# Storing w_in's blocks later, loading the second batch's first groups earlier, and v's first block behind them

## The chip, the cores and the metric

One Trainium2 chip, of which the kernel uses one core. The core has five engines with an instruction stream each (PE multiplies matrices, DVE, ACT and POOL work on vectors, SP issues the transfers) and 16 DMA engines. The metric is device time in microseconds (us), from the start to the end of one execution; lower is better.

## The reference

```python
def _attn_ref(q, k, v, tau):                      # B, N, C = 4, 6080, 256
    qn = q / (norm(q, axis=1) + 1e-06)            # over the N rows, for each channel
    kn = k / (norm(k, axis=1) + 1e-06)
    s = kn.transpose(0, 2, 1) @ qn / tau          # 256 x 256 for each batch
    a = softmax(s)                                # rows of s
    return v @ a

def _moe_ref(x, w_in, w_out):                     # x: the 4 * 6080 rows of v @ a
    h = x @ w_in                                  # d_ff = 2048
    g = h - tanh(h)
    return g @ w_out                              # back to 256 channels
```

## The kernel before

For each batch the kernel computes the 256x256 scores of k against q over all 6080 rows, the softmax, and then folds the result into the weights: (v @ a) @ w_in is computed as v @ (a @ w_in). w_in is cut into 8 blocks (s = 0 to 7) of 256 columns; "fold" multiplies a by one block (tiles `ps_w`), and the folded block `f` is used for all of v. The product v @ f is done by seven half-size products (a Strassen scheme; tiles `x`, `y`, `z` collect them), then tanh and the subtraction follow on ACT and DVE (`t`, `gh`, `gl`), and the product with w_out (`ps_o`). Numbers that need more than one pass are held as a high and a low part (`_hi`, `_lo`, `eh` and `el`, `gh` and `gl`), and products are sums of three.

**The start**, to which all of the change belongs. The first batch's scores are 48 steps of 128 rows over 25 groups (group 0 has one step, the last a half-filled one, all others two). A group is one load of q and k, into whichever tiles are unused that early: `vhl`, `gh`, `gl`, `qh`, `ql`. PE multiplies them (`ps_s`), ACT squares them in place, DVE and POOL add the squares up (`acc`). Then come, one behind the other: the sum of the squares over the rows on PE (`ps_n`, 24 short matmuls), the norms on DVE, their spread (`ps_b`), the scaled scores and their maximum (`s`, `nmx` on DVE), the exponentials on ACT, the transposition on PE (`ps_t`), its high and low part (`eh` on ACT, `el` on DVE), the fold of block 0 (`ps_w`), its scaling and splitting (`fx`, `f`), and then the first seven products with v (`x`). v's first block is one load `vraw_0` of 1 MB; ACT and DVE make the seven pairs `v` (through sums `vt`) out of it.

**What PE does meanwhile.** The second batch's scores are there to fill PE: the first `FILLS` = 48 steps of them ("fills") are put wherever PE would have to wait. In the traces they too are `ps_s`. Their groups are loaded into two tiles `qh` (even groups) and two tiles `ql` (odd groups), so that the load of `qh_4` has to wait until the matmuls on `qh_0` are done.

**The weights.** w_in and w_out come as 64-bit numbers. Each of their blocks (eight and eight) is loaded as `raw` (three tiles in turn) and converted: `L331` on ACT, `L336` to `L346` on DVE (`a_wi`, `m_wi`, `a_wo`, `m_wo`), one addition and one subtraction on POOL or DVE, and a cast on ACT. The converted blocks of w_in are stored to memory for the later batches (`wi_d`, `keep_w_in`, L376); blocks 0 to 2 stay in tiles `wi` until their fold, blocks 3 to 6 are converted in tiles that `f` needs later, and are loaded back.

**What sets the order.** The program is a list of operations. A planner (`Plan.order`) gives each an estimated start from costs and dependences and writes them out in that order; on each engine they run strictly in this order. An operation can have a due time, which only decides which of several ready ones comes first, and `after`, which only delays its estimated start: on the chip there is no wait for either. What an instruction does wait for is data and tiles that come free. All transfers are issued by SP, one after the other, on one queue; an issue that waits for a tile holds up all that stand behind it.

```python
LEAD = 6
KEPT = 50.0
FIRST = 3
...
        if i == len(steps) - LEAD:
            scored.append(plan.last_pe)
...
            size=0.26 * groups[g][1], after=scored if b else (), ...
```

`scored` is the matmul of the first batch's scores behind which the planner lets the second batch's first load start, and until now v's first load too (`plan_moving(0, scored)`). `kept[s]` is the store of block s.

Of the kernel before, what the change touches and what calls it, by code (L numbers as in the profile page):

```python
# [37 lines left out]
EARLY = 6  # L38
FILLS = 48
FILL_EVERY = 0.6  # L40
LEAD = 6
KEPT = 50.0
FIRST = 3
PAD = 208
# [167 lines left out]
def act_cost(n):  # L212
    return 0.14 + n * 0.0009


def dve_cost(n):
    return 0.157 + n * 0.00104
# [11 lines left out]
def attn_moe(ctx: ExitStack, tc: tile.TileContext, qk, v4, qkT, tau, w_in, w_out, outT):  # L229
# [43 lines left out]
    def bank(i, name, shape=(P, 512)):  # L273

        return ps_p.tile(list(shape), F32, tag=f"bank{i}", name=name)
# [6 lines left out]
    def products(out, terms, first, last):  # L282

        seq = []
        for (wh, wl), (xh, xl) in terms:
            seq += [(wh, xh)] if wl is None else [(wh, xl), (wh, xh), (wl, xh)]
        for i, (w, x) in enumerate(seq):
            ins = nc.tensor.matmul(  # L288
                out, w, x,
                start=first and i == 0, stop=last and i == len(seq) - 1,  # L290
                skip_group_check=True,
            )
        return ins
# [63 lines left out]
    wi = {}  # L357
# [6 lines left out]
    def convert_w_in(s, tag):  # L364
        def dst():
            if tag == "f":
                f = sb(f_p, "f", [P, 2, NS, P], F32R, f"w_{s}").rearrange("p a n f -> p (a n f)")
                w = wi[0, s] = f[:, 0:2 * KC * FB].rearrange("p (a k f) -> p a k f", a=2, k=KC)
            else:
                w = w_in_tile(0, s)  # L370
            return w[:, 0].rearrange("p k f -> p (k f)"), w[:, 1].rearrange("p k f -> p (k f)")

        return Convert(f"wi{s}", w_in[s], dst)

    def keep_w_in(s):
        nc.sync.dma_start(wi_d[s], wi[0, s].bitcast(F32))  # L376
# [22 lines left out]
    class Attn:  # L399
# [208 lines left out]


        def fold(self, s, i):  # L610
            w = wi.pop((self.b, s))
            pw = self.pw[s] = bank(i, f"ps_w_{self.b}_{s}", (P, KC, FB))
            for m in range(KC):
                ms = slice(m * P, (m + 1) * P)
                products(
                    pw[:, m, :],
                    [((self.eh[:, kk, ms], self.el[:, kk, ms]), (w[:, 0, kk, :], w[:, 1, kk, :])) for kk in range(KC)],
                    first=m == 0, last=m == KC - 1,
                )
# [79 lines left out]
    plan = Plan()  # L699
# [22 lines left out]
    def plan_convert(conv, dst, after=(), due=None, alone=False):  # L722

        adds = ("DVE", dve_cost(WN), nc.vector) if alone else ("POOL", pool_cost(WN), nc.gpsimd)
        raw, c, t = Buf(ring["raw"]), Buf(ring["nt"]), Buf(ring["ob"])
        plan.add("SP", 0.35, conv.load, writes=[raw, dst], after=after, size=0.52, due=due)
        plan.add("ACT", act_cost(WN), conv.magnitude, reads=[raw], writes=[c])
        plan.add("DVE", 0.84 + 0.69, conv.upper, reads=[raw], writes=[c])
        plan.add("DVE", 0.42 + 0.69, conv.lower, reads=[raw, c], writes=[t])
        plan.add(*adds[:2], lambda: conv.add(adds[2]), reads=[t], writes=[c])  # L730
        plan.add("ACT", act_cost(WN), conv.hi, reads=[c], writes=[dst])
        plan.add(*adds[:2], lambda: conv.lo(adds[2]), reads=[c], writes=[dst])

    kept = {}

    def plan_w_in(s, due=None, tag="wi", after=(), alone=False):
        w = wbuf[0, s] = Buf(ring[tag])
        plan_convert(convert_w_in(s, tag), w, after, due, alone)
        w.writers[-1].due = plan.pe_time - 0.5
        kept[s] = plan.add("SP", 0.35, lambda: keep_w_in(s), reads=[w], size=0.52, due=plan.pe_time + (KEPT if s < FIRST else 0.0))  # L740

    def plan_load_w(b, s):
        w = wbuf[b, s] = Buf(ring["wi"])
# [6 lines left out]
    def plan_moving(i, after=()):  # L750
        v = moving[i] = Moving(i // NP, i % NP)
        n = v.n
        raw, t = Buf(ring["vraw"]), Buf(ring["vt"])
        plan.add("SP", 0.35, v.load, writes=[raw], after=after, size=1.05)
        for j in range(3):
            plan.add("DVE", dve_cost(n if j else 2 * n), lambda j=j: v.sums(j), reads=[raw], writes=[t])
        vbuf[i] = {}
        for j in range(7):
            h = Buf(ring["vhl"])
            l = Buf(f"vl{i}_{j}", h)  # L760
            src = t if v.PLACES[j][0] else raw
            plan.add("ACT", act_cost(n), lambda j=j: v.split_hi(j), reads=[src], writes=[h])
            plan.add("DVE", dve_cost(n), lambda j=j: v.split_lo(j), reads=[src, h], writes=[l])
            vbuf[i][j] = h, l
# [294 lines left out]
    scored = []  # L1059
# [8 lines left out]
    def plain_step(b, i, due=None):  # L1068
        g, jj = steps[i]
        if jj == 0:  # L1070
            plain_load(b, g)

        return plan.add("PE", 2 * KC * 0.215, lambda: ats[b].score(g, jj), reads=held[b, g], writes=[scores[b]], due=due, fill=b == 1)
# [23 lines left out]
    for i, (g, jj) in enumerate(steps):  # L1097
        if jj == 0 and g in early:
            plan_w_in(early[g], due=plan.pe_time, tag="wi" if early[g] < FIRST else "f")
        if i == len(steps) - LEAD:  # L1100
            scored.append(plan.last_pe)
        plain_step(0, i)
        if jj == groups[g][1] - 1:
            plain_square(g)
        if i == 8:
            pt = Buf(1)
            plan.add("PE", 0.1, spread_tau, reads=[tau_b], writes=[pt])
            plan.add("DVE", 0.2, take_tau, reads=[pt], port=False)
    after_scores = plan.pe_time

    fills = [plain_step(1, i, after_scores + FILL_EVERY * i) for i in range(FILLS)]

    sq, pn = [Buf(ring["u"]) for _ in range(2)], Buf(1)
    for x in range(2):
        plan.add("ACT", act_cost(GJ * C), lambda x=x: ats[0].take_squares(x), reads=acc[x:x + 1], writes=sq[x:x + 1])
    plan_moving(0, scored)
    plan.add("PE", 12 * 0.22, lambda: ats[0].sum_squares(1), reads=sq + acc[2:], writes=[pn], late=1.0)
    norms, spread, softmax, transpose = plan_softmax(ats[0], pn, scores[0])
    norms()
# [4 lines left out]
    plan_fold(0, 1, 1)  # L1124
    plan_fold(0, 2, 3)
    plan_w_in(EARLY, due=after_scores, tag="f")
    for s in range(NS2):
        plan_convert(convert_w_out(s), wobuf[s], due=after_scores + 10.0 * s, alone=s > 0)
    for s in range(FIRST, NS2):
        task(max(s - 4, 0), "start", lambda s=s: plan_w_in(s, after=[plan.last_pe], alone=True) if s > EARLY else plan_load_w(0, s))  # L1130
# [90 lines left out]
```

## Time and profile before

| | |
|---|---|
| Median of 3 runs | 2171.91 us (2171.20 to 2172.46) |
| Profiled execution, its own time | 2172.06 us |
| Its span | 2170.3 us |
| PE busy | 2160.4 us |
| DVE busy | 1750.3 us |
| ACT busy | 1529.9 us |
| POOL busy | 33.0 us |
| Mean granted TensorE clock | 0.998 of full speed |

The span is the time between the first and the last instruction in the profiled execution; its own time is 1.76 us longer and can be compared with the runs. A busy PE is not always a PE at its full pace: the granted clock has to be read beside it.

### The profile page before, as it was taken

How to read it: one execution, taken by the hardware profiler on the slowest of the kernel's cores; microseconds unless marked ns; L12 is line 12 of the kernel's file. 1: busy time of each engine (PE TensorE's matmuls, PEld its weight loads, DVE VectorE, ACT ScalarE, POOL GpSimd, SP SyncE). 2: the span in 40 equal slices, each digit the busy share in tenths (PEclk: the TensorE clock that was granted, in tenths of full speed). 3: DMA queues.
4: the chain of work that ended last, by engine and by line, in shares of the span. 5: the costliest groups of instructions: out<-in, count | busy, mean ns of one | idle time of the engine just before them, and what ended most of it. 6: DMA issues, size and time to landing. Idle time of an engine off the chain costs nothing.

```text
span 2170.3 us, 28452 instructions
## 1 busy us (share of the span) xinstructions
PE 2160.4 (100%) x10042; PEld 1818.0 (84%) x10042; DVE 1750.3 (81%) x2844; ACT 1529.9 (70%) x2755; POOL 33.0 (2%) x31
## 2 busy tenths in 40 slices
PE   8999999999999999999999999999999999999999
PEld 7888888888888888888888888888888888888887
DVE  8888877888888777778788877877878878778776
ACT  6566778776777777776677767777667766666665
POOL 5100000000000000000000000000000000000000
PEclk9999999999999999999999999999999999999999
DMA  9844444443454444543345445454333342332331
GB/s 389 330 166 154 164 168 148 162 154 105 151 209 151 172 164 168 182 160 140 126 145 187 170 162 189 143 189 167 128 134 128 122 148 88 129 129 93 125 120 53
DMA packets 82783, 342.23 MB, mean 158 GB/s; under 512 B 9042, under 2 KB 13138, under 8 KB 80082
## 3 DMA queue, kind: packets, MB, share of 16 engines
q1 hardware_dynamic: 82642, 340.43, 43.3%
q8 instruction: 79, 1.29, 0.2%
q14 instruction: 62, 0.51, 0.1%
HBM read 281.94 MB, written 58.46 MB: 157 GB/s over the span
## 4 chain that ended last, share of the span: by engine, by line
PE 98%; DMA 1%; DVE 0%; SPq 0%; issue 0%; ACT 0%
PE ps_o L905 48%; PE x L288 24%; PE y L288 12%; PE ps_s L288 6%; PE z L288 6%; PE ps_w L288 2%; DMA qh<-qk_dram 0%; DMA vhl<-qk_dram 0%; PE ps_n L457 0%; DVE m_wi L346 0%; PE ps_b L564 0%; PE ps_t L599 0%; DVE acc L445 0%; DVE a_wi L339 0%; SPq L323 0%
## 5 line engine op out<-in xcount | busy, mean ns | idle before, releaser
L288 PE MATMUL x<-v,f 128*128 128x512 f32 (+1 forms) x2304 | 614.9, 388 | 0.0
L905 PE MATMUL ps_o<-gh,wo_h 128*128 128x512 f32 (+1 forms) x1536 | 596.8, 389 | 0.0
L905 PE MATMUL ps_o<-gh,wo_l 128*128 128x512 f32 (+1 forms) x1536 | 596.3, 388 | 0.0
L845 DVE TENSOR_TENSOR gl<-t,gh 128x512 fp32r<-128x512 f32 (+1 forms) x768 | 513.1, 681 | 57.3 <-ACT gh L841 55.3
L841 ACT CAST gh<-t 128x512 fp32r<-128x512 f32 (+1 forms) x768 | 463.7, 617 | 68.5 <-DVE t L837 61.2
L288 PEld LDWEIGHTS x<-v,f 128*128 128x128 f32 x2304 | 432.4, 188 | 87.4 <-issue 0.3
L905 PE MATMUL ps_o<-gl,wo_h 128*128 128x512 f32 (+1 forms) x1536 | 472.7, 389 | 0.0
L833 ACT ACTIVATE t<-c 128x512 f32<-128x512 f32 (+1 forms) x576 | 361.3, 628 | 134.0 <-DVE c L821 128.8
L837 DVE TENSOR_TENSOR t<-c,t 128x512 f32<-128x512 f32 (+1 forms) x576 | 392.5, 683 | 76.6 <-ACT t L833 69.0
L805 ACT COPY u<-x 128x512 f32<-128x512 f32 (+1 forms) x384 | 223.9, 583 | 236.7 <-PE x L288 235.7
L905 PEld LDWEIGHTS ps_o<-gh,wo_l 128*128 128x128 f32 x1536 | 288.5, 188 | 56.6 <-ACT gh L841 0.2
L905 PEld LDWEIGHTS ps_o<-gl,wo_h 128*128 128x128 f32 x1536 | 288.6, 188 | 55.3
L905 PEld LDWEIGHTS ps_o<-gh,wo_h 128*128 128x128 f32 x1536 | 288.7, 188 | 53.3
L821 DVE TENSOR_TENSOR c<-u,y 128x512 f32<-128x512 f32 (+1 forms) x384 | 261.0, 680 | 85.1 <-ACT u L805 51.4
L288 PE MATMUL y<-v,f 128*128 128x512 f32 (+1 forms) x1152 | 322.1, 388 | 0.0
L288 PEld LDWEIGHTS y<-v,f 128*128 128x128 f32 x1152 | 216.2, 188 | 43.1
L833 ACT ACTIVATE t<-x 128x512 f32<-128x512 f32 (+1 forms) x192 | 113.9, 593 | 114.7 <-PE x L288 113.5
L837 DVE TENSOR_TENSOR t<-x,t 128x512 f32<-128x512 f32 (+1 forms) x192 | 131.6, 685 | 72.9 <-ACT t L833 71.1
L821 DVE TENSOR_TENSOR c<-p,z 128x512 f32<-128x512 f32 (+1 forms) x192 | 130.9, 682 | 69.9 <-PE z L288 65.8
L288 PE MATMUL z<-v,f 128*128 128x512 f32 (+1 forms) x576 | 161.2, 388 | 0.0
L288 PEld LDWEIGHTS z<-v,f 128*128 128x128 f32 x576 | 108.1, 188 | 21.5
L805 ACT COPY p<-x 128x512 f32<-128x512 f32 (+1 forms) x192 | 112.0, 584 | 11.3 <-PE x L288 8.8
(122 smaller groups left out, 1490.4 us busy)
## 6 DMA issues: line engine op xcount, KB each, us to landing
f<-f_d SPq DMA_DIRECT2D x160, 896.0 KB, 4.6
nt<-qkT_dram SPq DMA_DIRECT2D x96, 380.0 KB, 5.7
f_d<-f SPq DMA_DIRECT2D x32, 896.0 KB, 3.8
raw<-qk_dram SPq DMA_DIRECT2D x46, 512.0 KB, 5.5
vraw<-v_dram SPq DMA_DIRECT2D x20, 1024.0 KB, 7.8
outT_dram<-ob SPq DMA_DIRECT2D x80, 256.0 KB, 3.1
wi<-wi_d SPq DMA_DIRECT2D x28, 512.0 KB, 5.4
vhl<-qk_dram SPq DMA_DIRECT2D x14, 512.0 KB, 8.9
```

Of the source, the lines that this page charges most:

```text
L288: ins = nc.tensor.matmul(out, w, x, start=first and i == 0, stop=last and i == len(seq) - 1, skip_group_check=True,)
L805: nc.scalar.copy(self.tiles[to], self.tiles["X"][:, 0:self.n])
L821: nc.vector.tensor_add(self.tiles[i], self.tiles[u], self.tiles[ps][:, 0:self.n])
L833: nc.scalar.activation(self.tiles["t", i], self.tiles[c][:, 0:n], AF.Tanh)
L837: nc.vector.tensor_sub(x, self.tiles[c][:, 0:n], x)
L841: nc.scalar.copy(self.g[i][0], self.tiles["t", i])
L845: nc.vector.tensor_sub(self.g[i][1], self.tiles["t", i], self.g[i][0].bitcast(F32))
L905: nc.tensor.matmul(outs[key + (m,)][:, 0:n], (wo_l if part else wo_h)[:, f, m * P:(m + 1) * P], quad.g[i][x], start=first and j == 0, stop ...
```

## The change

The converted blocks 3 to 7 of w_in get the same late due time for their store as blocks 0 to 2 had (50 us of planned PE time later). `fold` no longer takes the tile out of the list, since a store may now be written out behind the fold. The second batch's first load may be planned behind the matmul that stands nine steps before the scores' end, not six. v's first load is planned behind the ninth fill (`fills[8:9]`).

```diff
-LEAD = 6
+LEAD = 9
...
         def fold(self, s, i):
-            w = wi.pop((self.b, s))
+            w = wi[self.b, s]
...
-        kept[s] = plan.add("SP", 0.35, lambda: keep_w_in(s), reads=[w], size=0.52, due=plan.pe_time + (KEPT if s < FIRST else 0.0))
+        kept[s] = plan.add("SP", 0.35, lambda: keep_w_in(s), reads=[w], size=0.52, due=plan.pe_time + KEPT)
...
-    plan_moving(0, scored)
+    plan_moving(0, fills[8:9])
```

On SP, around the second batch's first load `qh_0` (names are those of the tiles, the number at the end counts tiles; `raw_wo` and `raw_wi` are loads of blocks to convert). Before:

```order
L323 DMA raw_wo_370<-w_out_dram 128x1024
L376 DMA wi_d_96<-wi_0_111 128x1024
L376 DMA wi_d_97<-wi_1_117 128x1024
L323 DMA raw_wo_395<-w_out_dram 128x1024
L323 DMA raw_wi_403<-w_in_dram 128x1024
L465 DMA qh_0_413<-qk_dram 128x512
L465 DMA ql_1_418<-qk_dram 128x1024
L465 DMA ql_3_428<-qk_dram 128x1024
L376 DMA wi_d_100<-w_241 128x1024
L465 DMA qh_2_445<-qk_dram 128x1024
L376 DMA wi_d_101<-w_291 128x1024
L674 DMA vraw_0_459<-v_dram 128x2048
```

And now:

```order
L323 DMA raw_wo_363<-w_out_dram 128x1024
L376 DMA wi_d_96<-wi_0_111 128x1024
L376 DMA wi_d_99<-w_199 128x1024
L376 DMA wi_d_97<-wi_1_117 128x1024
L465 DMA qh_0_395<-qk_dram 128x512
L465 DMA ql_1_399<-qk_dram 128x1024
L323 DMA raw_wo_408<-w_out_dram 128x1024
L465 DMA ql_3_417<-qk_dram 128x1024
L323 DMA raw_wo_427<-w_out_dram 128x1024
L376 DMA wi_d_98<-wi_2_149 128x1024
L465 DMA qh_2_447<-qk_dram 128x1024
L465 DMA qh_4_454<-qk_dram 128x1024
```

Two loads of weights that stood ahead of `qh_0` now stand behind `ql_1` or later (the load of w_in's block 6, `raw_wi`, much later), the store `wi_d_99` has come from further up to just ahead of `qh_0`, and three transfers have come between `ql_3` and `qh_2`.

On SP again, further down, where `vraw_0` stands now:

```order
L376 DMA wi_d_101<-w_299 128x1024
L323 DMA raw_wi_498<-w_in_dram 128x1024
L465 DMA qh_6_506<-qk_dram 128x1024
L465 DMA ql_7_527<-qk_dram 128x1024
L465 DMA qh_8_539<-qk_dram 128x1024
L674 DMA vraw_0_544<-v_dram 128x2048
L323 DMA raw_wo_554<-w_out_dram 128x1024
L465 DMA ql_9_558<-qk_dram 128x1024
```

It has moved from ahead of `qh_4` to behind `qh_8`, and with one more load of weights it stands between `qh_8` and `ql_9`.

On ACT, from the copies `sq` of the summed squares to the high part `eh` of the transposed exponentials. Before:

```order
L331 ACTIVATE a_wo_452<-raw_wo_395 128x512
L449 COPY sq_461<-acc_0_124 128x512
L449 COPY sq_464<-acc_0_125 128x512
L352 CAST wo_h<-a_wo_430 128x512
L693 CAST v_0_0_527<-vraw_0_459 128x512
L693 CAST v_0_0_529<-vraw_0_459 128x512
L693 CAST v_0_0_535<-vraw_0_459 128x512
L571 COPY rq<-ps_b_550 128x256
```

And now:

```order
L331 ACTIVATE a_wo_460<-raw_wo_408 128x512
L449 COPY sq_464<-acc_0_124 128x512
L449 COPY sq_467<-acc_0_125 128x512
L352 CAST wo_h<-a_wo_429 128x512
L331 ACTIVATE a_wo_537<-raw_wo_427 128x512
L571 COPY rq<-ps_b_551 128x256
L586 ACTIVATE s,sums<-s,nmx 128x256
L352 CAST wo_h<-a_wo_460 128x512
L693 CAST v_0_0_593<-vraw_0_544 128x512
L586 ACTIVATE s,sums<-s,nmx 128x256
L693 CAST v_0_0_600<-vraw_0_544 128x512
L693 CAST v_0_0_605<-vraw_0_544 128x512
```

The casts of v have moved from ahead of the copy `rq` to around the second exponential; the first of them stands ahead of it. The copies `sq` still stand behind the conversion of the second block of w_out, whose load now stands behind `ql_1`.

## Rows read from the trace of the kernel before

**Rows 1.** The page: the span, and the chain that ended last, by engine.

```profile
span 2170.3 us, 28452 instructions
...
PE 98%; DMA 1%; DVE 0%; SPq 0%; issue 0%; ACT 0%
```

**Rows 2.** PE's waits in the whole span: total us, times, longest us.

```profile
PE ps_s L288 <- DMA vhl<-qk_dram: 4.6, 3, 3.6
PE ps_s L288 <- DMA qh<-qk_dram: 1.5, 1, 1.5
```

**Rows 3.** Stretches: length, busy time of PE, PEld, DVE, ACT, POOL; clock, DMA share, GB/s.

```profile
49.20:50.80 1.60, 0.07 (x2) 0.03 (x1) 1.60 (x4) 1.60 (x4) 1.52 (x2) 1.00 1.04 412
...
51.00:54.40 3.40, 3.40 (x9) 2.67 (x9) 3.26 (x6) 0.42 (x1) 1.34 (x2) 0.52 1.03 423
54.40:57.90 3.50, 3.50 (x29) 3.37 (x28) 1.59 (x3) 0.50 (x1) 1.27 (x1) 0.98 1.03 425
57.90:61.10 3.20, 3.20 (x8) 2.50 (x9) 2.83 (x11) 1.52 (x4) 1.27 (x1) 0.51 1.00 411
...
6.00:63.00 57.00, 54.44 (x243) 46.04 (x243) 51.60 (x93) 36.52 (x49) 29.30 (x23) 0.94 1.03 412
63.00:80.00 17.00, 17.00 (x100) 15.55 (x99) 14.44 (x31) 6.59 (x15) 1.28 (x1) 1.00 0.87 293
```

**Rows 4.** The chain that ended last, around 40 to 58 us: start, us, what.

```profile
40.77 1.65 DVE m_wi L346
...
42.90 7.83 DMA qh<-qk_dram
...
55.32 2.57 PE ps_n L457 x24
57.89 7.84 PE ps_s L288 x28
```

**Rows 5.** Transfers issued from 33 to 63 us: count, KB each, median us to landing.

```profile
raw_wo<-w_out_dram SPq DMA_DIRECT2D x3, 512.0 KB, 8.4
ql<-qk_dram SPq DMA_DIRECT2D x3, 512.0 KB, 8.6
...
vraw<-v_dram SPq DMA_DIRECT2D x1, 1024.0 KB, 10.8
```

**Rows 6.** ACT in order of time: start, us, what [idle before, releaser].

```profile
49.82 0.65 ACT L331 ACTIVATE a_wo<-raw_wo 128x512 f32<-128x512 f32 x1
50.37 1.05 ACT L449 COPY sq<-acc 128x512 f32<-128x512 f32 x2
...
59.70 1.66 ACT L693 CAST v<-vraw 128x512 fp32r<-128x512 f32 x3 [1.68 <-DMA vraw<-v_dram]
...
70.04 0.51 ACT L586 ACTIVATE s<-s,nmx 128x256 f32<-128x256 f32 x1 [0.88 <-DVE nmx L583]
```

**Rows 7.** POOL and DVE in order of time.

```profile
48.39 4.03 POOL L445 TENSOR_TENSOR acc<-vhl,acc 128x512 f32<-128x512 f32 x3
...
55.33 0.69 DVE L346 SCALAR_TENSOR_TENSOR m_wo<-raw_wo,m_wo 128x512 f32<-128x512 uint32 x1
```

**Rows 8.** SP in order of time: the issue of the second batch's group 8.

```profile
64.90 0.33 SPq L465 DMA_DIRECT2D qh<-qk_dram  x1
```

**Rows 9.** PE in order of time: the first fill, and fills ahead of the first product.

```profile
50.78 1.75 PE L288 MATMUL ps_s<-qh 128*128 128x256 f32 x4 [1.53 <-DMA qh<-qk_dram]
...
68.60 1.89 PE L288 MATMUL ps_s<-ql 128*128 128x256 f32 x8
70.33 1.03 PE L288 MATMUL ps_s<-qh 128*128 128x256 f32 x4
...
72.50 1.89 PE L288 MATMUL ps_s<-ql 128*128 128x256 f32 x8
74.04 0.59 PE L288 MATMUL ps_w<-wi,eh 128*128 128x256 f32 x2
...
81.80 1.04 PE L288 MATMUL x<-v,f 128*128 128x512 f32 x3
```

## The prediction

> **What bounds the kernel now.** I read the chain of work that ended last before anything else. PE has 98% of it [rows 1]: whatever does not shorten PE's waits or its slow stretches changes nothing. Next, who waits for whom on PE. In the whole span PE waited in two places, 4.6 us in the first microseconds (for the first batch's groups) and 1.5 us once for `qh` [rows 2]. The change begins behind the first, so the second is the one within its reach. The chain in order of time shows where it lies: the first fill starts at 50.78 after a wait of 1.53 us [rows 9], so the first batch's scores end at 49.25. The load it waits for was issued at 42.90 and took 7.83 us [rows 4]. It could not be issued sooner because a load of w_in that stood ahead of it waited for its tile until DVE's conversion ended at 40.77 + 1.65 = 42.42 [rows 4].
>
> Then stretch by stretch, with the granted clock beside the busy time [rows 3]. The clock is at full speed in the wait itself, and at 0.52 and 0.51 in two stretches behind: 51.0 to 54.4, right after the wait, and 57.9 to 61.1, right after the 24 short matmuls of `ps_n`, which end at 57.89 [rows 4]. Those are the levels of 2.4 and 1.2 GHz. They cost 3.4 x 0.48 = 1.63 us and 3.2 x 0.49 = 1.57 us. So what there is to win around the change is 1.53 + 1.63 + 1.57 = 4.73 us, 0.22% of the time, and no more.
>
> Last, the transfers. From 6 to 63 us the DMA engines are full (share 1.03, 412 GB/s); from 63 to 80 they are at 0.87 [rows 3]. A load of 512 KB issued between 33 and 63 us lands 8.4 to 8.6 us later, the 1 MB of v 10.8 us later [rows 5]; at 412 GB/s 512 KB take 1.27 us, so each stands behind some six others. In this stretch a load's landing is decided by the bytes that stand ahead of it, hardly by when it is issued.
>
> **The change, part by part.** I follow the queue of SP as it stands now and give each 512 KB 1.27 us.
>
> The first fill. Ahead of `qh_0` two loads of weights are gone, so it lands 2 x 1.27 = 2.54 us sooner, at 50.73 - 2.54 = 48.2, a microsecond before the scores end. The tile that held SP up until 42.42 is no longer waited for ahead of it. PE's 1.53 us go. The store `wi_d_99` was ahead of `qh_0` before too. `ql_1` lands at 49.5, and is needed one step later, at 49.25 + 0.86 = 50.1 (two steps take 70.33 - 68.60 = 1.73 us [rows 9]): no wait. With the gap goes, I take it, the half-clock stretch that begins right behind it: 1.63 us.
>
> One rule speaks against that. The Trainium skill (TensorE: Matmul & The Clock Gate, Part 1: The HAM clock gate) lets the clock fall to half after the engine was idle for a whole period of observation; by it a wait with work on both sides would not do, the stretch would have some other cause and stay, and the sum below would be 1.63 us higher. The rows show the fall 0.2 us after the wait and none before [rows 3], so I go with them; that it stays is a rival below.
>
> The squares. `ps_n` follows three steps of fills, which now end at 49.25 + 2.59 = 51.84. It needs the two copies `sq` on ACT, and these stand behind the conversion of a block of w_out that now is loaded behind `ql_1`: it lands at 49.5 + 1.27 = 50.7. The conversion takes 0.65 us and the copies 1.05 us [rows 6], so `ps_n` starts at 52.5: a new wait of 0.6 us. If the load lands 0.6 us sooner it is nothing; if each of the three queued pieces ahead takes a tenth more, 1.0. POOL's last addition ended at 48.39 + 4.03 = 52.42 [rows 7] and has one conversion less ahead of it now, so it is no later than ACT.
>
> Group 2. `ps_n` takes 2.57 us [rows 4] and ends at 55.0. The next fill needs `qh_2`, and between `raw_wo_408` and it stand `ql_3`, a load of w_out and a store: 50.7 + 4 x 1.27 = 55.8. A new wait of 0.8 us, from nothing (if the queue runs 4% faster from 6 us on) to 1.6 (if one more transfer's time is lost). The tile of `qh_2` was free at POOL's word before the queue reaches it, so the bytes decide. The second half-clock stretch follows `ps_n` before and will now too, from about 54.6. Some of it falls on the wait, where a slow clock costs nothing: of 1.57 us I take 0.4 off; between 1.57 less (it does not come) and 1.6 more (a further one comes) the row of the same work is the nearest.
>
> v and group 9. From the start of group 2 PE had 72.50 - 57.89 = 14.6 us of work to group 9, in the same order as now [rows 4, 9]; less 0.4 for the clock it is there at 55.8 + 14.2 = 70.0. The queue: 55.8, then eight transfers of 512 KB to `qh_8` (10.2 us) make 66.0, v's 1 MB 68.5, a load of w_out and `ql_9` 71.1. A new wait of 1.0 us. The same time holds for the chain beside it: the second exponential now stands behind the first cast of v on ACT, so 68.5 + 0.6 for the cast [rows 6] + 0.7 for the exponential puts the transposition at 69.8, about where PE is. The wait is between nothing (the queue catches up while SP waits for tiles) and 2.2 us (behind 63 us the DMA share was 0.87 [rows 3]: 13% of the eight microseconds up to 71.1 on top). Behind SP's wait for the tile of `qh_8`, which frees with the matmuls on `qh_4` (issue at 64.90 before [rows 8], about 62.5 now), stand v, a load of w_out and `ql_9`; PE, ACT and DVE all wait for these.
>
> Behind it. The first product `x` came at 81.80 [rows 9]; the fills ahead of it are one step more now, so it is hidden unless v's seven pairs are late: some 3.6 us of DVE behind `el`, against 4.3 us of folds and three steps of fills on PE. The stores cost nothing: nobody waits for the blocks until the loads back, whose place in the queue is hardly moved. Conversions of w_out come at the same pace, and the host's change in `fold` issues nothing. The last 2,000 us are as before.
>
> The sum: -1.53 - 1.63 + 0.6 + 0.8 - 0.4 + 1.0 = -1.2 us. The profiled execution's own time is 2172.06 us, so 2170.9; the median of the runs is 0.15 us below it, which makes 2170.7. With the waits at their bounds and the second stretch as it is, the likeliest case reaches from 2169.3 to 2172.0.
>
> **The rivals.**
> 1. The data is in time. SP issues `qh_2` to `ql_9` while the queue has fewer bytes in it, and the three new waits vanish: -1.53 - 1.63 = -3.2, 2168.7 us. The share of 0.87 behind 63 us speaks for some slack, the 1.03 before it against.
> 2. A half-clock stretch too many. Either the one behind the wait stays though the wait is gone, or the new wait ahead of group 9, added to the one for the transposition, comes near the 1.53 us that stood ahead of a fall before, and a third stretch follows: +1.6 on the forecast, 2172.3 us, no change at all. For it: rows of a fall after 1.53 us [rows 3]. Against it: the new waits are shorter, each taken alone.
> 3. v is late, and the kernel slower. If v lands later than 68.5, the first cast holds up the second exponential, the transposition, `el` and the folds one for one, since all fills ahead of them are done; `ql_9` is late with it. More than 1.2 us later (behind 69.7) and the gain is gone, and a wait so long has the half clock behind it: at 2 us late +2.0 + 1.6 on the forecast, 2174.3 us. It passes 0.2% (which is about what a measurement of this kernel can tell from none, 4.3 us) when v lands 4 us late. For it: v stands behind a wait for `qh_4`'s matmuls; against it: SP's issue comes 6 us ahead of the landing that I count with.
> 4. Both stretches go. Without the gap the clock does not fall behind `ps_n` either: up to -1.53 - 1.63 - 1.57 = -4.7, 2167.2 us. Against it: nothing in `ps_n` changes.
>
> **How the numbers follow.** The forecast has 0.50, rivals 1 to 4 have 0.16, 0.20, 0.11 and 0.03. The predicted time is the forecast's, 2170.7 us. Rival 1 with its own spread and rival 2 lie inside 2168.3 to 2173.8; outside are rival 4 and the worse half of rival 3, with some of the tails, less than 0.2. Faster by over 0.2% (below 2167.6) needs rival 4 or rival 1 with luck: 0.04. Slower by over 0.2% (above 2176.2) needs v 4 us late: 0.06. The rest, 0.90, is within 0.2%.
>
> **What would show it.** PE's waits: no wait for `qh` at 49.25, one of about half a microsecond ahead of `ps_n`, one of about 0.8 us for `qh` behind it, one of about 1 us around `ps_t` and the fill after it. The granted clock: full from 50 to 54 us, half for some 3 us from about 55, full again up to 75. ACT's first cast of v waits for `vraw` and starts at about 68.5. Group 0 lands at about 48.2. Wrong would be: a half-clock stretch before 54 us without a wait, a wait of over 2 us at `ps_t`, or any PE wait behind 85 us (a load back of w_in, a store that a fold's tile waits for), which I count at nothing.

## The result, and the profile after

The changed kernel takes 2175.0 us (median of 22 runs, 2173.2 to 2177.2), the kernel before 2171.9 us (22 runs, 2170.5 to 2172.6): a ratio of 1.0015, with a 95% interval of 1.0008 to 1.0022. That is slower by 0.15%, less than the 0.2% set as the bound, but clear of 1. The forecast was 2170.7 us within 2168.3 to 2173.8: the time lies above the range, and the change went the other way. The profiled execution took 2174.89 us, 2.83 us more than the one before; its span is 2.5 us longer than in [rows 1].

The page: the span and the chain by engine, as in [rows 1].

```profile
span 2172.8 us, 28456 instructions
...
PE 98%; DMA 1%; DVE 0%; issue 0%; POOL 0%; ACT 0%
```

PE's waits in the whole span (total us, times, longest us), beside [rows 2]:

```profile
PE ps_s L288 <- DMA vhl<-qk_dram: 3.5, 1, 3.5
PE ps_s L288 <- DMA ql<-qk_dram: 0.9, 1, 0.9
PE ps_t L599 <- ACT s L586: 0.8, 1, 0.8
PE ps_s L288 <- DMA qh<-qk_dram: 0.3, 1, 0.3
```

The wait of 1.5 us for `qh` has gone. Three others are new, 2.0 us together: 0.3 for `qh`, 0.8 for the second exponential, 0.9 for `ql`. The 1.1 us less in the first microseconds bring almost nothing: the first fill starts at 49.08, where the scores ended at 49.25 before.

PE in order of time from the first fill to the first product (start, us, what, [idle before, releaser]), beside [rows 9]:

```profile
49.08 1.13 PE L288 MATMUL ps_s<-qh 128*128 128x256 f32 x4
...
51.96 0.87 PE L457 MATMUL ps_n<-ones,sq 128*128 128x1 f32 x4
...
56.08 3.78 PE L288 MATMUL ps_s<-qh 128*128 128x256 f32 x8 [0.27 <-DMA qh<-qk_dram]
...
71.10 0.38 PE L599 MATMUL ps_t<-ident,s 128*128 128x128 f32 x2
72.27 0.44 PE L599 MATMUL ps_t<-ident,s 128*128 128x128 f32 x2 [0.79 <-ACT s L586]
73.56 2.81 PE L288 MATMUL ps_s<-ql 128*128 128x256 f32 x8 [0.86 <-DMA ql<-qk_dram]
...
77.52 0.83 PE L288 MATMUL ps_w<-wi,eh 128*128 128x256 f32 x2
...
85.51 1.04 PE L288 MATMUL x<-v,f 128*128 128x512 f32 x3
```

The same stretch by windows, with the columns of [rows 3] (the clock is the third number from the end):

```profile
54.20:60.90 6.70, 6.43 (x19) 5.34 (x20) 6.28 (x18) 1.28 (x2) 2.53 (x2) 0.50 0.99 398
...
61.10:74.50 13.40, 11.76 (x58) 9.99 (x57) 9.01 (x20) 5.00 (x12) 0.00 (x0) 1.00 0.92 343
74.50:74.90 0.40, 0.40 (x3) 0.29 (x3) 0.40 (x1) 0.40 (x2) 0.00 (x0) 0.62 1.01 410
74.90:78.20 3.30, 3.30 (x11) 2.67 (x10) 3.30 (x7) 0.90 (x2) 0.00 (x0) 0.53 0.97 338
78.20:100.00 21.80, 21.80 (x120) 19.23 (x119) 16.96 (x35) 14.87 (x28) 3.11 (x2) 1.00 0.75 273
```

The first half-clock stretch of [rows 3] has gone with its wait. The second, behind the squares, now lasts 6.7 us in place of 3.2. A third, which was not there before, follows the waits for the exponential and for `ql`.

SP's issues in order of time, where `qh_8` is the third row and v the fourth:

```profile
59.88 0.33 SPq L465 DMA_DIRECT2D qh<-qk_dram  x1
62.21 0.33 SPq L465 DMA_DIRECT2D ql<-qk_dram  x1
63.94 0.33 SPq L465 DMA_DIRECT2D qh<-qk_dram  x1
64.32 0.43 SPq L674 DMA_DIRECT2D vraw<-v_dram  x1
64.85 0.37 SPq L323 DMA_DIRECT2D raw_wo<-w_out_dram  x1
65.67 0.33 SPq L465 DMA_DIRECT2D ql<-qk_dram  x1
```

v's load in the answer on its tile (issue between two times, then the time to landing):

```profile
L674 SPq DMA_DIRECT2D vraw<-v_dram x1: 426/426/426, 64.3 to 64.3; - x1
...
DMA to landing us min/median/max: 6.8/6.8/6.8
```

And ACT, at the block of w_out ahead of the squares and at the first cast of v:

```profile
50.75 0.68 ACT L331 ACTIVATE a_wo<-raw_wo 128x512 f32<-128x512 f32 x1 [0.93 <-DMA raw_wo<-w_out_dram]
51.34 1.05 ACT L449 COPY sq<-acc 128x512 f32<-128x512 f32 x2
...
71.09 0.62 ACT L693 CAST v<-vraw 128x512 fp32r<-128x512 f32 x1 [2.19 <-DMA vraw<-v_dram]
71.62 0.50 ACT L586 ACTIVATE s<-s,nmx 128x256 f32<-128x256 f32 x1
```

v is issued at 64.32, right behind `qh_8`, and lands 6.8 us later at 71.1. ACT, strictly in order, waits 2.19 us for it with the second exponential behind, and PE's transposition waits for that. PE starts on `ql_9`, issued at 65.67, at 73.56.

### The profile page after: what moved, and what is told of

Read it like the earlier page. It is cut to its first block, busy times and chain, and to the rows that moved or that the text cites. A ratio compares the mean times of both kernels' runs of the same rounds, so it can differ in the third digit from the quotient of the medians.

```text
span 2172.8 us, 28456 instructions
## 1 busy us (share of the span) xinstructions
PE 2163.4 (100%) x10042; PEld 1820.6 (84%) x10042; DVE 1748.9 (80%) x2844; ACT 1530.1 (70%) x2755; POOL 33.1 (2%) x31
## 3 DMA queue, kind: packets, MB, share of 16 engines
q8 instruction: 79, 1.29, 0.2%
## 4 chain that ended last, share of the span: by engine, by line
PE 98%; DMA 1%; DVE 0%; issue 0%; POOL 0%; ACT 0%
PE ps_o L905 48%; PE x L288 24%; PE y L288 12%; PE ps_s L288 6%; PE z L288 6%; PE ps_w L288 2%; DMA qh<-qk_dram 0%; DMA ql<-qk_dram 0%; DMA vhl<-qk_dram 0%; DVE acc L445 0%; DVE m_wi L346 0%; DVE a_wi L339 0%; PE ps_b L564 0%; PE ps_t L599 0%; POOL w L355 0%
## 5 line engine op out<-in xcount | busy, mean ns | idle before, releaser
L905 PEld LDWEIGHTS ps_o<-gl,wo_h 128*128 128x128 f32 x1536 | 288.6, 188 | 55.3
```

Source lines behind the costliest of these rows:

```text
L905: nc.tensor.matmul(outs[key + (m,)][:, 0:n], (wo_l if part else wo_h)[:, f, m * P:(m + 1) * P], quad.g[i][x], start=first and j == 0, stop ...
```

## The experiments

Where did the loss come from? The expectations name these theories. **A**: v's late issue makes it, through ACT's wait, `ql_9` and the third half-clock stretch. **B**, the rival: the missing first wait makes it, since what the earlier data gives is given back by the longer half-clock stretch behind the squares. **C**, formed later: that stretch has a price of its own, apart from the waits. **D**, C's rival: a full clock there wins nothing, since the fills' loads set the pace or the added work takes it. All times are medians in us; "before" is the kernel before in the same series, and the interval is that of the ratio.

| run | this | before | ratio, interval |
|---|---|---|---|
| e1_v_as_before | 2171.53 | 2172.11 | 0.9997, 0.9989 to 1.0006 |
| e2_v_alone | 2174.95 | 2172.11 | 1.0014, 1.0005 to 1.0023 |
| e3_lead_alone | 2172.01 | 2172.11 | 1.0000, 0.9991 to 1.0009 |
| e4_stores_alone | 2172.20 | 2172.11 | 1.0001, 0.9992 to 1.0010 |
| e5_dense_after | 2174.51 | 2171.84 | 1.0019, 1.0010 to 1.0027 |
| e6_dense_e1 | 2171.69 | 2171.84 | 1.0001, 0.9992 to 1.0009 |
| e7_v_behind_5 | 2171.45 | 2171.84 | 0.9999, 0.9990 to 1.0007 |
| e8_wo_later | 2173.55 | 2171.84 | 1.0006, 0.9998 to 1.0015 |
| e9_dense_ps_t | 2174.49 | 2171.76 | 1.0012, 1.0003 to 1.0020 |
| e10_v5_wo_late | 2171.65 | 2171.76 | 1.0000, 0.9991 to 1.0009 |
| e11_v7_wo_late | 2172.57 | 2171.76 | 1.0003, 0.9994 to 1.0012 |
| e12_half_dense_ps_t | 2173.45 | 2171.95 | 1.0009, 1.0000 to 1.0018 |
| e13_half_dense_e1 | 2170.46 | 2171.95 | 0.9995, 0.9986 to 1.0004 |
| e14_half_dense_e10 | 2170.50 | 2171.95 | 0.9995, 0.9986 to 1.0004 |
| e15_half_dense_e7 | 2171.05 | 2171.95 | 1.0000, 0.9992 to 1.0009 |

### The change without v's move, and each part alone

The changed kernel with v's first load where it was (e1):

```diff
-    plan_moving(0, fills[8:9])
+    plan_moving(0, scored)
```

> The changed kernel with v's first load planned as before (the store times and the lead of nine steps stay). Theory A: v standing behind group 8 is what costs, by the two waits around the transposition (0.8 and 0.9 us, with idle time of 1.6 us in all) and the half-clock stretch behind them (1.7 us): without it 3.3 us less than the changed kernel's 2175.0, about 2171.7 us, no PE wait at the transposition, full clock from 61 to 80 us. Rival B: the doubled half-clock stretch behind the squares (54.2 to 60.9 us) is what costs, and v's lateness is hidden in it: about 2174 to 2175 us.

The kernel before with v's move alone (e2, the same line the other way), with `LEAD = 9` alone (e3), and with the stores' due times and `fold`'s list alone (e4):

> The kernel before with v's first load alone moved behind the ninth fill. Theory A: v lands at about 71 us here too, the transposition and the fill after it wait, a half-clock stretch follows: 2171.9 + 3.3 = about 2175 us, with the 1.5 us wait for the first fill still there. Rival B: v's place costs nothing by itself, 2171.5 to 2172.5 us.

> The kernel before with the lead of nine steps alone. Theory A: the first fill's wait of 1.5 us and the half-clock stretch behind it go, the stretch behind the squares grows by some 1.6 us as in the changed kernel: about 2170.5 us. Rival B: the fills now outrun their loads and give all of it back: 2172 us or more. If the stretch behind the squares does not grow: 2168.7 us.

> The kernel before with the later due time of all stores alone. Theory A: the first fill still stands behind two loads of weights, so its wait stays: 2171 to 2172.5 us, no change that can be told. Rival B: the stores moved behind the first fills push group 2 back and lengthen the half-clock stretch behind the squares by up to 1.6 us: about 2173.5 us.

e1 comes out 0.6 us below the kernel before by its median, where the change came out 3.1 above; e2 has 2.84 us, about all of the loss. v's place makes it, as A has it, and B is out as the cause of the loss. e1's windows show that the long half-clock stretch is there without v's move too, and the third is not:

```profile
54.00:62.00 8.00, 7.31 (x23) 6.09 (x23) 7.31 (x18) 2.33 (x4) 2.54 (x2) 0.57 1.03 415
62.00:74.00 12.00, 11.70 (x57) 9.84 (x56) 9.07 (x23) 2.86 (x8) 0.81 (x1) 1.00 0.89 301
```

e3 missed A's number: the earlier first load alone brings nothing (0.1 us), although its profile has no wait at the first fill. It has two later ones, 0.6 for `qh` and 0.5 for `ql`, and a half-clock stretch of 3.5 us (55.3 to 58.8). By the median B is right so far: what the first wait gave is given back. How, this trace does not show, for its own run took 2170.83 us, 1.2 less than the profiled run of the kernel before. e4 moves nothing; the first fill waits there as before, 1.8 us.

e2 holds a surprise. Its first fill waits 1.29 us, and no half clock follows; first the wait's window, then the one behind it:

```profile
49.30:51.00 1.70, 0.41 (x3) 0.15 (x2) 1.70 (x4) 1.70 (x4) 1.62 (x2) 1.00 0.97 392
51.00:54.40 3.40, 3.29 (x18) 2.63 (x18) 3.30 (x6) 0.74 (x2) 1.67 (x2) 1.00 1.03 420
...
74.50:78.00 3.50, 3.50 (x15) 3.21 (x14) 2.90 (x5) 0.00 (x0) 0.00 (x0) 0.53 1.01 365
```

Behind its wait of 2.1 us for `ql_9` half clock does follow, as in the changed kernel. That wait is the only one that e2 has there:

```profile
70.82 0.60 PE L599 MATMUL ps_t<-ident,s 128*128 128x128 f32 x4
73.50 2.65 PE L288 MATMUL ps_s<-ql 128*128 128x256 f32 x8 [2.08 <-DMA ql<-qk_dram]
```

In e2 both exponentials stand ahead of the first cast of v on ACT, and the transposition waits for nothing. So A's route through ACT is not needed for the loss. `ql_9` was issued at 65.39 there and came 8.1 us later, behind v's 1 MB and a load of w_out; in e1, without v ahead of it, it was issued at 65.44 and PE started on it 5.8 us later.

### v two and three groups sooner, and the weights later

The changed kernel with v behind the fifth fill (e7: `fills[4:5]`, behind group 6), and with blocks 3 to 7 of w_out planned behind the eighteenth fill (e8):

```diff
-        plan_convert(convert_w_out(s), wobuf[s], due=after_scores + 10.0 * s, alone=s > 0)
+        plan_convert(convert_w_out(s), wobuf[s], due=after_scores + 10.0 * s, after=fills[17:18] if s > 2 else (), alone=s > 0)
```

> The changed kernel with v's first load planned behind the fifth fill, not the ninth: it stands behind group 6 on the queue, two groups sooner. Theory A (v's place costs by the tile it is queued behind): its issue moves from 64.3 to about 60.3 us and it lands at about 65, before the exponentials need ACT; no wait at the transposition, no half-clock stretch behind 74 us: about 2171.7 us. Rival: any place behind the fills costs the same, since the 1 MB stand ahead of the later groups: 2174 us or more, with PE waits for groups 7 to 9 in place of the ones at the transposition.

> The changed kernel with the load of w_out's fourth block planned behind the eighteenth fill, so that only v stands between groups 8 and 9. Theory A splits in two: the 0.8 us at the transposition (ACT's cast of v ahead of the second exponential) stays, the 0.9 us for group 9 goes (1.3 us fewer bytes ahead of it); if the half-clock stretch behind needs both waits, it goes too: about 2172.5 us; if the one wait is enough, about 2174 us. Rival: the block of w_out has no part in it, 2175 us.

In e7 v is issued at 60.98 and lands 5.8 us later; the transposition waits for nothing, and the whole loss is gone (2171.45). SP and PE in order of time:

```profile
60.98 0.33 SPq L674 DMA_DIRECT2D vraw<-v_dram  x1
...
72.36 0.60 PE L599 MATMUL ps_t<-ident,s 128*128 128x128 f32 x4
```

3.3 us of issue time, ahead of two waits for tiles (those of `ql_7` and `qh_8`), decide 3 us, though the stretch behind the squares is as long as in the changed kernel (6.9 us at 0.51). In e8 v is still issued at 64.07, behind the same tile, and lands at 72.6. Both halves of A's split were missed: the transposition does not wait, and PE waits 2.2 us for `ql_9`, which comes 8.4 us after its issue with v alone between it and `qh_8`. So the block of w_out is not what holds it. About half of the loss is gone all the same. In the profiled run no half clock follows that wait, and the stretch behind the squares has 2.8 us in place of 6.7, behind a wait of 1.4 us for `qh`; which of the two brings the gain was not parted.

```profile
68.00:74.00 6.00, 3.42 (x15) 2.36 (x15) 3.38 (x8) 2.07 (x6) 0.00 (x0) 1.00 0.98 384
74.00:80.00 6.00, 6.00 (x38) 5.54 (x39) 5.82 (x11) 3.90 (x9) 0.00 (x0) 1.00 0.97 379
```

Two versions with both, e10 (v at `fills[2:3]`, blocks 1 to 7 behind `fills[13:14]`) and e11 (`fills[4:5]`, blocks 2 to 7 behind `fills[11:12]`):

> A version that the runs so far point to: the changed kernel with v's first load behind group 5 (planned behind the third fill) and the loads of w_out's blocks 1 to 7 planned behind the fourteenth fill. The waits for the squares (0.2 to 0.5 us), at the transposition and for group 9 go. If these are what is left: 2170 to 2171 us. If the fills' loads ahead of group 6 stay the limit, since stores take the places of the loads moved: 2171.5 us as with v behind group 6.

> As the run before, but v behind group 6 (planned behind the fifth fill) and only w_out's blocks 2 to 7 later, behind the twelfth fill. It differs from the run with v behind group 6 alone by the blocks of w_out: if these cost anything on the queue, about 0.5 to 1 us below it (2170.5 to 2171 us), if not, the same 2171.5 us.

Both are level with the kernel before; e11's expectation was missed. Fewer bytes ahead of the loads do not take the waits for `qh` away (1.1 and 1.5 us).

### The clock, with PE kept busy

To price the half-clock stretches, products that nobody reads were put in. Behind each group of the squares' short matmuls (e5, e6 with `DENSE = 2`; e13 to e15 with 1):

```diff
+                    for _ in range(DENSE):
+                        nc.tensor.matmul(
+                            self.pn[:, 256:512], ones, self.acc[0][:, x, :],
+                            start=True, stop=True, skip_group_check=True,
+                        )
```

And behind each half of the first transposition (e9 with 4, e12 with 2):

```diff
+                for _ in range(2 if self.b == 0 else 0):
+                    nc.tensor.matmul(
+                        self.pb[:, 256:512], ones, self.e[:, 0, :],
+                        start=True, stop=True, skip_group_check=True,
+                    )
```

Each stands as two matmuls in the trace, which made e9's added work 3.5 us, twice what its expectation counts with.

The changed kernel (e5) and e1 (e6) with two products at the squares, and the changed kernel with four at the transposition (e9):

> The changed kernel with two unneeded 128x256 matmuls behind each three short ones of the squares' sum (eight more in all, some 3.5 us of PE at full clock, nothing reads them). Theory C: the half-clock stretch of 6.7 us behind the squares comes from the short matmuls, and with it PE gives the fills' tiles back late, so v's load is issued late (64.3 us): with PE kept busy there, the clock stays at 1.00 from 54 to 61 us, v is issued at 62 to 63 us, and the kernel ends 1 to 3 us below the changed one's 2175.0. Rival D: the clock falls anyway, or what is won goes into the added work: 2174.5 to 2177 us.

> The same eight unneeded matmuls in the kernel with v's load as before (2171.5 us). Theory C: the half-clock stretch (54 to 61.6 us there, some 3.7 us of work lost) goes and the fills start up to 2 us later: 2169.5 to 2170.5 us. Rival D: the fills are held up by their loads, not by the clock, and nothing is won: 2171.5 to 2173 us.

> The changed kernel with four unneeded 128x256 matmuls behind each half of the first batch's transposition (eight, 1.7 us at full clock, nothing reads them), where PE waits 0.8 and 0.9 us anyway. It parts the two things that v's late load costs. If half of the loss is the half-clock stretch behind those waits (1.7 us): the clock stays full from 74 to 78 us and the kernel ends at about 2173.3 us. If the waits and the chain behind them are all of it, or the clock falls anyway: 2175 to 2176 us.

e5 and e6 came out in D's ranges. But these three added as much work as the clock takes, so their times say little on C. In e9's profile the transposition does not wait and the clock is full from 61 to 78 us, but 3.5 us of added work stand against that. e6's clock is full throughout, and it is level with e1:

```profile
50.00:62.00 12.00, 12.00 (x68) 10.72 (x67) 8.70 (x19) 4.49 (x8) 3.85 (x4) 1.00 1.02 414
```

Eight runs of e5 had a mean granted clock of 1.000 and took 2173.9 to 2174.8 us. Against e6 that is some 2.6 us for v's place, measured with the long stretch out of the way on both sides: a second piece of evidence for A. The other four runs lost clock, and took 2175.7 to 2182.7 us. A mean clock of 1.000 leaves the eight no room for a third stretch either: one that costs 1.7 of 2174 us would bring the mean to 0.999.

With less added work: the changed kernel with two at the transposition (e12), and e1, e10 and e7 with one at the squares (e13, e14, e15):

> The changed kernel with two unneeded 128x256 matmuls behind each half of the first transposition (each runs as two in the trace: 1.7 us of PE in all, about as long as PE waits there). If the half-clock stretch behind is half of the loss and the filled waits keep the clock up: 1.7 us less than the changed kernel's 2175.0, about 2173.3 us. If the waits are all of the loss: 2175 us.

> v's load as before, the other two parts of the change kept, and one unneeded 128x256 matmul behind each group of short ones of the squares' sum (1.7 us of PE in all, 0.7 of it where PE waits for group 2 anyway). Theory C: the half-clock stretch behind the squares costs PE time of its own (3.7 us of work): if the clock holds, 2171.5 - 3.7 + 1.0 = about 2169 us. Rival D: the fills' loads set the pace there and the slow clock is hidden behind them: 2171 to 2172 us.

> The same four matmuls in the version with v behind group 5 and w_out's blocks later. Theory C: 2171.65 less some 1.5 us, about 2170 us. Rival D: 2171.5 to 2172.5 us.

> The same four matmuls in the version with v behind group 6. Theory C: 2171.45 less up to 2 us, about 2169.5 us. Rival D: 2171 to 2172 us.

In e12 the third stretch is gone, though the transposition still waits 0.6 us:

```profile
71.00:74.50 3.50, 2.88 (x16) 1.88 (x14) 2.44 (x5) 2.48 (x6) 0.00 (x0) 1.00 1.03 420
74.50:80.00 5.50, 5.50 (x36) 5.19 (x37) 5.34 (x10) 3.07 (x7) 0.00 (x0) 1.00 0.90 337
```

It takes 1.5 us less than the changed kernel, with 1.7 us of useless products in it that partly lie in the waits: by this run the third stretch is about half of the loss. By e5's eight runs, 2.6 us above e6 without it, the waits and the chain behind them can make most of the loss by themselves. How the loss divides between the two is not settled.

e13 missed C's 2169 us, but shows that the stretch has a price. Ten of its eleven runs have a mean clock of 1.000 and take 2170.0 to 2171.1 us; the profiled one has 0.998 and takes 2172.82, with the stretch in it:

```profile
54.50:61.50 7.00, 7.00 (x23) 5.88 (x23) 5.58 (x14) 1.82 (x4) 1.71 (x2) 0.53 1.00 408
```

The same instructions, so 2.4 us for 7 us at half clock (median 2170.46 to 2172.82). That is one run, but e15 has the same split: seven runs at 1.000 with a median of 2170.8 us, four at 0.998 with 2174.1, so 3.3 us. By their medians e14 is near C's 2170 us and e15 in D's range. e13 and e14 are 1.5 us below the kernel before by their medians, e15 0.9 below; their intervals reach over 1, so no version beat the kernel before beyond what was measured. The kernel before itself takes 2170.6 us in the median of its six runs at 1.000 (of 128 beside e1 to e15), so what e13 and e14 gain is about what a full clock gives. What e14 has left of waits behind the first microseconds is 0.6 us for DVE's `diag` and 0.2 for `el`.

## Why the prediction was wrong

| step | forecast, us | measured, us |
|---|---|---|
| wait of the first fill | -1.53 | -1.53 |
| half clock behind it | -1.63 | -1.63 |
| `ps_n` waits for `sq` | +0.6 | about +0.4 |
| wait for `qh_2` | +0.8 | +0.27 |
| half clock behind the squares | -0.4 | 6.7 x 0.50 - 1.57 = +1.8 |
| v and group 9, waits | +1.0 | 13.40 - 11.76 = +1.64 |
| a third half-clock stretch | 0 | 0.4 x 0.38 + 3.3 x 0.47 = +1.70 |
| sum | -1.2 | +2.6 |

From the scores' end to the first product it took 36.4 us, and 32.55 before [rows 9], where one step of 0.86 us less lay ahead of the product: 3.0 us more, of which the rows above name 2.6 (with some 0.1 twice, since the wait of 0.27 lies inside the 6.7 us). The earlier end of the scores gives back 0.17; the 0.35 that are left to the 2.5 of the span come back behind the product, by the difference alone.

**What held.** The queue's arithmetic was right as long as the queue was full. `qh_0` was forecast to land at 48.2 and did (issue at 39.26, 8.9 us). The block of w_out came at 50.75 (forecast 50.7), and `qh_2` at 56.0 (55.8). The wait and the half clock right behind it went as forecast. `ps_n` started at 51.96 (forecast 52.5), but its first four matmuls took 0.87 us, where they took 0.50 in the kernel before: I read the wait for the second copy as lying in them. (Two transfers stand between `ql_3` and `qh_2` now, not three as the section on the change has it; the prediction counted two.) No load back of w_in and no store made a wait behind 85 us, and e4 agrees that the stores cost nothing that can be told. None of the three signs of being wrong that the prediction names came; what gave it away is in its list of what should be seen, ACT's first cast of v at 71.09 us in place of 68.5 and a stretch of 6.7 us in place of some 3.

**First failure: "v and group 9".** The step counted bytes to the end: v at 68.5 behind eight transfers. It says itself that SP's wait for `qh_4`'s matmuls stands ahead, put at 62.5, and takes this for harmless. The fills ahead of them ran at half clock until 60.9, so the tile came free at 63.9. With SP's issues held up the queue ran low: from 60 to 66 us the DMA share is 0.81, at 240 GB/s.

```profile
60.00:66.00 6.00, 6.00 (x29) 5.19 (x28) 3.05 (x8) 0.00 (x0) 0.00 (x0) 0.92 0.81 240
```

So v's landing went by its issue plus 6.8 us, not by the bytes ahead, and came 2.6 us late: 1.8 by the issue (64.32 for 62.5), 0.8 by the time to landing (6.8 for 6.0). `ql_9` behind it, forecast at 71.1, came at 73.56. That is rival 3's mechanism, which gave 2174.3 us for 2 us late and had 0.11. The half clock behind such waits, which rival 2 had on its own, came with it. The two were counted as separate cases; they are one chain. e1, e2 and e7 show it (v's place alone makes the loss, two groups sooner takes it away), and e12 gives the third stretch half of it.

**Second failure: "of 1.57 us I take 0.4 off".** The half clock behind the squares became twice as long. It was neither shortened by the wait nor near "the row of the same work". The bound of the step, 1.6 more for a further stretch, was about the truth (1.8). That stretch also helped the first failure along, since PE's work towards freeing SP's tile runs in it. In e1 it costs 8.0 x 0.43 = 3.4 us, as much as both stretches of before together (1.63 + 1.57), which is why the change without v's move gains so little. Why it lasts 3.2 us before, 3.5 in e3 and some 7 in e1, e7 and the changed kernel was not settled. Added products prevent it in most runs (all of e6 and e14 and ten of e13's eleven have a mean clock of 1.000, but only seven of e15's eleven), and with one kernel and one order it comes in some runs and not in others (e13, e15), so the order of the work alone does not set it.

**The rule on the clock.** The prediction took the rows' side: a fall after a wait of 1.53 us. The runs show that a wait's length does not tell. Half clock followed 1.53 us in the kernel before and 0.8 and 0.9 us with short work between in the changed one; none followed 1.29 us in e2 and 2.2 us in e8. By the Trainium skill (TensorE: Matmul & The Clock Gate, Part 1: The HAM clock gate) the clock falls when the engine has been idle, and the periods in which it is watched run on regardless of the kernel, so that it also depends on where in one the work lies. The second half agrees with the split of e13's and e15's runs. The first half does not agree with the stretch behind the squares: PE counts as busy before it, in `ps_n`'s one-column matmuls [rows 3, 4].

## What to carry to other kernels

A load that is moved behind an issue which waits for a tile inherits the pace of the work that frees that tile: forecast its landing twice, by the bytes ahead and by the issue plus a landing time, and take the later. Do the same for the loads that it now stands ahead of, as `ql_9` here. Where a wait and a slow clock can set each other off, they are one case and not two, and half-clock stretches belong in the sum with an honest range. Of three edits made together one did all the harm (stores 0.1 us, first loads -0.1, v 2.8), so each is worth a run by itself.

## What the runs showed of the hardware

The granted clock differs between runs of one program by more than the changes under study are worth: e13 at 1.000 and at 0.998 are 2.4 us apart, e15 3.3. The kernel before shows it too, in its 128 runs beside e1 to e15: 2170.6 us in the median at 1.000 (6 runs), 2171.2 at 0.999 (47), 2172.2 at 0.998 (71) and 2173.7 at 0.997 (4). So differences of 0.1% are to be read with the mean granted clock of the runs beside them. And once at half, the clock stayed there for 10.4 us in e5's profiled run, though PE was counted busy without a gap:

```profile
55.00:65.40 10.40, 10.40 (x33) 8.75 (x32) 3.47 (x17) 1.27 (x2) 2.53 (x2) 0.51 0.56 227
```
